# Compact head operands, padded on chip: the operand staging of an attention and MLP training kernel

## The chip, the cores and the metric

The kernel runs on one core of one Trainium2 chip. The metric is the device time of one execution in microseconds (us). A run is an execution of its own, and a kernel's time is the median of its runs.

Engines are named as the profile names them: PE is the matrix engine (PEld its weight loads), DVE the vector engine, ACT the scalar engine, POOL is GpSimd, SP is the engine that only issues DMAs. The recorded texts also say VectorE for DVE, ScalarE for ACT, GpSimd for POOL and SyncE for SP. ACTq and SPq are the instructions by which ACT and SP issue DMAs. PSUM is where this kernel's matmuls put their results, and an *eviction* is the copy of such a result by DVE or ACT to a tile that other operations or DMAs read. The *granted clock* of PE is the share of its full clock that the profile shows as let through.

## The reference, cut to what matters

The reference computes the output and all gradients of one block that multiplies attention by a gate from an MLP:

```python
x  = A_x                                  # [1, 2048, 512] bf16
xn = layernorm(x)
q, k, v = split(xn @ wqkv)                # 32 heads of 16 columns
s  = softmax(q k^T / 4) v @ wo            # attention
g  = silu(gelu(layernorm(xn) @ w1 + b1) @ w2 + b2)   # MLP, 1792 wide
out = x + s * g
# returned: out and the gradients of x, wqkv, wo, w1, b1, w2, b2 for a given grad_out
```

## The kernel before

The kernel has three parts. The *preparation* normalizes x, computes K and V, then Q, then the MLP with its gate, and projects the gradient of the attention output through `wo` (`do_proj`). The *attention* works on 16 pairs of heads, in 4 blocks of queries with 16 steps each, 1024 steps in all. The *gradient part* does the rest.

The attention wants, for each pair, K with V, Q, and the projected gradient (call it DO) with columns on partitions. The kernel before gets these by DMA transposes that read a scratch in DRAM. In that scratch each pair has 128 columns per tile of 128 rows: two heads of 64, each holding `1 or -norm | 16 columns | 16 columns | 31 zeros`. So the preparation fills two staging tiles `KP` with zeros once, writes the live columns into them, and stores them whole, zeros too, 1 MB for two tiles of rows.

```python
# K/V stage (two KP tiles, used in turn)
KP = [stg.tile([128, NPAIR, 2, 128], bf16, name=f"KP{i}") for i in range(2)]
for i in range(2):
    nc.gpsimd.memset(KP[i][:], 0.0)
    ...
for t in range(NT):                       # 16 tiles of 128 rows
    ...                                   # 8 matmuls: pk, pv
    nc.vector.tensor_copy(out=kpv[:, :, :, 1:17], in_=pk...)
    nc.scalar.copy(out=kpv[:, :, :, 17:33], in_=pv...)
    if t % 2 == 1:
        (nc.sync if (t // 2) % 2 == 0 else nc.scalar).dma_start(out=k.KVsrc[...], in_=kp[:])
    nc.vector.tensor_tensor(out=sq..., in0=kk, in1=kk, op=ALU.mult)     # squares of K
    nc.vector.reduce_sum(out=kn2[:], in_=sq[:], axis=AX.X)
    nc.vector.tensor_tensor(out=kmaxrun[:], in0=kmaxrun[:], in1=kn2[:], op=ALU.max)
nc.gpsimd.partition_all_reduce(kmax2[:], kmaxrun[:], channels=128, reduce_op=bass_isa.ReduceOp.max)

# Q stage: the same two tiles
QP = KP
for i in range(2):
    nc.gpsimd.memset(QPv[:, :, :, :, 17:33], 0.0)
for t in range(NT):
    ...                                   # 4 matmuls: pq; cast into QP; copy to NQ; squares, sum, norm
    if t % 2 == 1:
        (nc.sync if (t // 2) % 2 == 0 else nc.scalar).dma_start(out=k.QTsrc[...], in_=qp[:])

# MLP stage, once per tile t of 128 rows (ps_m: 14 matmuls)
nc.vector.tensor_tensor(out=m_bf[:], in0=pm[:], in1=b2bc[:], op=ALU.add)
nc.scalar.activation(out=sg[:], in_=m_bf[:], func=ACT.Sigmoid)
nc.vector.tensor_tensor(out=gB[:, 0, :], in0=m_bf[:], in1=sg[:], op=ALU.mult)
nc.scalar.dma_start(out=dot[:], in_=go2[t * 128:(t + 1) * 128, :])
nc.vector.tensor_tensor(out=dso[:], in0=dot[:], in1=gB[:, 0, :], op=ALU.mult)
...                                       # dso to DRAM; transposed by PE, copied to dsoT by ACT
nc.gpsimd.tensor_scalar(out=q[:], in0=sg[:], ...)      # three POOL operations
nc.gpsimd.tensor_tensor(out=q[:], in0=q[:], in1=gB[:, 0, :], op=ALU.mult)
nc.gpsimd.tensor_tensor(out=q[:], in0=q[:], in1=sg[:], op=ALU.add)
nc.vector.tensor_tensor(out=gB[:, 1, :], in0=q[:], in1=dot[:], op=ALU.mult)
nc.scalar.dma_start(out=k.GB_s[t * 128:(t + 1) * 128, :, :], in_=gB[:])
if t >= 1:
    do_proj(t - 1)

def do_proj(t):
    ...                                   # 4 matmuls: pd
    nc.vector.tensor_copy(out=dpv[:, :, :, 17:33], in_=pd...)
    nc.scalar.copy(out=nd[:, :, t % 4, :]..., in_=pd...)
    if t % 4 == 3:
        nc.scalar.dma_start(out=k.NATQd_s[...], in_=nd[:])
    if t % 2 == 1:
        (nc.sync if (t // 2) % 2 == 0 else nc.scalar).dma_start(out=k.DOTsrc[...], in_=dp[:])

# attention, operands of one pair (all issued by SP)
eng.dma_start_transpose(out=t["KVT"]..., in_=KVT_s[p]...)   # from KVsrc in DRAM
eng.dma_start_transpose(out=t["QT"]...,  in_=QT_s[p]...)
eng.dma_start_transpose(out=t["DOT"]..., in_=DOT_s[p]...)
...                                       # three plain loads
```

The program text is not the order of execution on an engine. A scheduler in the build puts the instructions of each engine into one fixed sequence, and the engine then runs that sequence in order.

## Time and profile before

The time before was 3028.48 us, the median of four runs (3026.97 to 3030.4). The profiled execution took 3025.2 us.

The table of windows of the kernel before gives one row per stage, cut at events read from the timeline: first K/V eviction, last K tile, last Q tile, first matmul of the MLP's second layer (`ps_m`), last eviction of `pd`, first `gts` (the first full attention step), last `acc` (end of attention). Evictions are those by DVE. The columns are start and end of the window, its length, busy time and number of instructions of PE, PEld, DVE, ACT and POOL, the granted PE clock as a share of full speed, the busy share of the DMA engines, and GB/s.

```profile
67.00:104.10 37.10, 30.44 (x126) 13.10 (x129) 31.51 (x67) 9.27 (x17) 8.60 (x5) 0.88 0.78 214
104.10:155.80 51.70, 26.27 (x88) 9.85 (x90) 39.01 (x89) 19.83 (x40) 1.43 (x2) 0.79 0.71 187
155.80:176.50 20.70, 17.54 (x76) 7.66 (x75) 14.71 (x23) 14.95 (x24) 6.96 (x2) 0.86 0.68 216
176.50:305.20 128.70, 101.67 (x455) 44.08 (x463) 70.83 (x110) 49.77 (x80) 50.76 (x50) 0.91 0.54 163
305.20:323.60 18.40, 2.50 (x12) 0.82 (x14) 0.02 (x1) 3.91 (x4) 0.34 (x2) 0.50 1.09 270
323.60:2421.60 2098.00, 1894.21 (x16637) 562.20 (x16634) 1545.61 (x1664) 1936.39 (x2046) 195.06 (x574) 1.00 0.82 148
2421.60:3025.20 603.60, 412.83 (x2370) 212.25 (x2410) 299.69 (x419) 163.72 (x259) 259.23 (x224) 0.87 0.39 119
```

Attention is 69% of the span, and ACT is busy 92% of it (1936 of 2098 us). The change acts before attention, in some 320 us. There no engine is busy all through a row; DVE comes nearest in the first (31.51 of 37.10 us), and PE in the third (17.54 of 20.70). The fifth row, the start of attention, is 18.4 us in which nearly nothing computes.

The list of waits of the kernel before, for 60 to 156 us, shows what the K/V and Q stages wait for. Columns: engine, what it was about to write and on which line, what released it; total us, number of waits, longest.

```profile
POOL KP L156 <- DMA KVsrc<-KP: 28.1, 1, 28.1
ACT NQ L167 <- DVE KP L164: 21.6, 9, 5.1
PE pq L160 <- DVE KP L164: 19.4, 6, 9.2
...
DVE KP L164 <- DMA QTsrc<-KP: 10.4, 4, 4.0
...
POOL kmax L151 <- DVE sqq L171: 6.1, 1, 6.1
```

POOL's zero fill of the tiles for Q waits for the last K/V writes (the 28.1 us are POOL's idle time, mostly free). PE waits 19.4 us for DVE to evict Q, and DVE waits 10.4 us for the 1 MB writes that still read the two staging tiles.

### The profile page before, as it was taken

The numbers are of one execution on the slowest core, as the hardware profiler recorded it, in microseconds if no ns is written. First come the engines' busy times: TensorE is split into PE (matmuls) and PEld (weight loads), VectorE is DVE, ScalarE is ACT, GpSimd is POOL, SyncE is SP. The second block draws the span as 40 slices with busy tenths as digits, with TensorE's granted clock in tenths as the row PEclk, the third lists the DMA queues.
The fourth block names the chain that finished last, engine by engine and source line by source line (L and its number), as shares of the span: only waits on it lengthen the run. The fifth ranks groups of instructions, "written<-read, shape, count | busy, mean of one in ns | idle before, by whom it ended". The sixth has DMA issues, their size and how long they took to land. (4 is left out here: it accounts for less than half of the span.)

```text
span 3025.2 us, 50085 instructions
## 1 busy us (share of the span) xinstructions
PE 2506.4 (83%) x19909; PEld 864.8 (29%) x19968; DVE 2035.1 (67%) x2470; ACT 2217.1 (73%) x2503; POOL 523.5 (17%) x867
## 2 busy tenths in 40 slices
PE   3678698998998998998998999899899865665967
PEld 2233222222222222222222222222222233332443
DVE  5855577777777777777777777777777637882034
ACT  2344699999999999999999999999999924441020
POOL 1043001001001001001001001001000126881024
PEclk8889899999999999999999999999999988887989
DMA  5855978878887887878788798878867663325431
GB/s 168 218 178 171 186 139 155 149 146 163 130 166 146 148 151 143 166 134 161 147 147 159 135 167 142 152 147 147 163 131 136 105 220 105 102 81 149 129 124 42
DMA packets 1365582, 442.27 MB, mean 146 GB/s; under 512 B 1247714, under 2 KB 1349475, under 8 KB 1365347
## 3 DMA queue, kind: packets, MB, share of 16 engines
q1 hardware_dynamic: 1267186, 374.04, 63.7%
q10 hardware_dynamic: 98160, 65.02, 7.2%
q8 instruction: 156, 2.56, 0.4%
q14 instruction: 80, 0.65, 0.1%
HBM read 69.34 MB, written 76.03 MB: 48 GB/s over the span
## 5 line engine op out<-in xcount | busy, mean ns | idle before, releaser
L698 DVE TENSOR_TENSOR gts<-d,et 128x1024 bf16<-128x1024 f32 x1024 | 1251.9, 1223 | 547.7 <-ACT et L687 524.2
L687 ACT ACTIVATE et<-s 128x1024 bf16<-128x1024 f32 x1024 | 1050.2, 1026 | 163.4 <-PE s L644 128.4
L724 ACT ACTIVATE e<-t 128x1024 bf16<-128x1024 f32 x1024 | 1049.7, 1026 | 6.3 <-PE t L656 5.1
L656 PE MATMUL t<-KVT,QT 64*128 64x512 bf16 x2048 | 400.8, 379 | 127.0 <-ACT e L724 122.6
L820 PE MATMUL Z<-e,W 128*32 128x512 bf16 x2048 | 396.2, 381 | 45.9 <-POOL W L787 45.9
L667 PE MATMUL d<-DOT,KVT 64*128 64x512 bf16 x2048 | 401.1, 380 | 18.0 <-DVE gts L698 9.3
L644 PE MATMUL s<-QT,KVT 64*128 64x512 bf16 x2048 | 401.3, 388 | 13.8 <-DMA QT<-QTsrc 12.4
L739 PE MATMUL X<-et,Lc 128*32 128x512 bf16 x2048 | 403.3, 389 | 2.4 <-DVE xt L772 0.4
L824 PE MATMUL Z<-gk,W 128*32 128x512 bf16 x2048 | 400.5, 379 | 0.0
L755 PE MATMUL X<-gts,NAT 128*17 128x512 bf16 x2048 | 395.6, 381 | 0.0
L742 PE MATMUL X<-et,NAT 128*32 128x512 bf16 x2048 | 395.2, 391 | 0.0
L781 POOL TENSOR_TENSOR W<-NATQ,rL 128x128 bf16<-128x128 bf16 x64 | 25.7, 402 | 1892.2 <-DVE rL L780 1892.2
L656 PEld LDWEIGHTS <-QT 64*128 64x128 bf16 x2048 | 179.1, 94 | 374.2 <-issue 373.9
L667 PEld LDWEIGHTS <-KVT 64*128 64x128 bf16 x2048 | 180.8, 93 | 265.1 <-issue 249.1
L644 PEld LDWEIGHTS <-KVT 64*128 64x128 bf16 x2048 | 100.9, 93 | 441.8 <-issue 440.3
L739 PEld LDWEIGHTS <-Lc 128*32 128x32 bf16 x2048 | 100.5, 93 | 243.9 <-issue 235.5
L820 PEld LDWEIGHTS <-W 128*32 128x32 bf16 x2048 | 118.9, 96 | 107.0 <-POOL W L787 64.4
L832 DVE TENSOR_TENSOR acc<-Z,acc 64x512 f32<-64x512 f32 x192 | 129.2, 673 | 8.7 <-PE Z L824 8.7
L824 PEld LDWEIGHTS <-W 128*32 128x32 bf16 x2048 | 105.6, 96 | 76.6 <-issue 3.3
L755 PEld LDWEIGHTS <-NAT 128*17 128x17 bf16 x2048 | 94.6, 88 | 11.5 <-issue 4.9
L742 PEld LDWEIGHTS <-NAT 128*32 128x32 bf16 x2048 | 95.0, 94 | 1.1 <-issue 1.1
L437 PE MATMUL dh_tp<-ident_bf,dh 128*128 128x128 bf16 x224 | 29.2, 263 | 77.1 <-DVE dh L434 74.7
(198 smaller groups left out, 2548.2 us busy)
## 6 DMA issues: line engine op xcount, KB each, us to landing
NAT<-KVsrc SPq DMA_DIRECT2D x16, 512.0 KB, 4.5
gk<-gts SPq DMA_TRANSPOSE x512, 4.3
HG_s<-hg SPq DMA_DIRECT2D x16, 448.0 KB, 2.8
DH_s<-dh ACTq DMA_DIRECT2D x16, 448.0 KB, 2.5
KVsrc<-KP SPq DMA_DIRECT2D x4, 1024.0 KB, 5.7
KVsrc<-KP ACTq DMA_DIRECT2D x4, 1024.0 KB, 5.7
QTsrc<-KP SPq DMA_DIRECT2D x4, 1024.0 KB, 5.2
QTsrc<-KP ACTq DMA_DIRECT2D x4, 1024.0 KB, 8.0
```

What stands on the lines that cost most here:

```text
L644: nc.tensor.matmul(s[:, hj, :], lhsT=op["KVT"][r0:r0 + 64, kb * 128:(kb + 1) * 128], rhs=op["QT"][r0:r0 + 64, qc * 512:(qc + 1) * 512], st ...
L656: nc.tensor.matmul(t[:, hj, :], lhsT=op["QT"][r0:r0 + 64, q0:q0 + 128], rhs=op["KVT"][r0:r0 + 64, kc * 512:(kc + 1) * 512], start=True, st ...
L667: nc.tensor.matmul(d[:, hj, :], lhsT=op["KVT"][r0:r0 + 64, kb * 128:(kb + 1) * 128], rhs=op["DOT"][r0:r0 + 64, qc * 512:(qc + 1) * 512], s ...
L687: nc.scalar.activation(out=et, in_=st_s.pop(g)[:], func=ACT.Exp)
L698: nc.vector.tensor_tensor(out=gts[:, kb % 2], in0=st_d.pop(g)[:], in1=st_et[g], op=ALU.mult)
L724: nc.scalar.activation(out=e[:], in_=st_t.pop(g)[:], func=ACT.Exp)
L739: nc.tensor.matmul(X[64 + 32 * hj:64 + 32 * hj + 32, :], lhsT=Lc[:, :], rhs=et[:, hj, :], start=(kb == 0), stop=False, skip_group_check=Tr ...
L742: nc.tensor.matmul(X[32 * hj:32 * hj + 32, :], lhsT=NATt[:, kb, 64 * hj + 1:64 * hj + 33], rhs=et[:, hj, :], start=(kb == 0), stop=(kb == ...
L755: nc.tensor.matmul(X[64 + 32 * hj:64 + 32 * hj + 17, :], lhsT=NATt[:, kb, 64 * hj:64 * hj + 17], rhs=gts[:, kb % 2, hj, :], start=False, s ...
L820: nc.tensor.matmul(Z[32 * hj:32 * hj + 32, :], lhsT=W1[:, qb, hj, :], rhs=erhs, start=(qb == 0), stop=False, tile_position=(0, 32 * hj))
L824: nc.tensor.matmul(Z[32 * hj:32 * hj + 32, :], lhsT=W2[:, qb, hj, :], rhs=grhs, start=False, stop=(qb == 3), tile_position=(0, 32 * hj))
L832: nc.vector.tensor_tensor(out=av, in0=Z[0:64, :], in1=av, op=ALU.add)
```

## The change

The intent is to keep the zeros out of DRAM. K/V, Q and DO go to DRAM compact; the attention loads them compact, copies them into padded tiles on chip, and transposes from there.

1. K/V: two staging tiles of four row tiles, 33 columns per head instead of 64. A write is 1.08 MB for four row tiles instead of 2 MB, in runs of 528 bytes. K is evicted by ACT, V by DVE, and the squares move from DVE to ACT. The big zero fill is gone. The pool of the small work tiles gets a third buffer (`p15_wk`).
2. Q: four staging tiles instead of the two shared ones, 17 columns per head, runs of 272 bytes; no second, padded copy; evicted by ACT.
3. `do_proj`: the padded eviction and the 1 MB `DOTsrc` writes are dropped. DVE makes the compact copy that ACT made.
4. Attention: three padded tiles, filled by POOL copies, and transposes from them; a third `NAT` buffer (K with V, rows on partitions); the PSUM pools of X and Z are put ahead of that of d.

The diff, cut to its core:

```diff
-            wk = c0.enter_context(tc.tile_pool(name="p15_wk", bufs=2))
+            wk = c0.enter_context(tc.tile_pool(name="p15_wk", bufs=3))
-            KP = [stg.tile([128, NPAIR, 2, 128], bf16, name=f"KP{i}") for i in range(2)]
+            NS = [stg.tile([128, NPAIR, 4, 2, NATW], bf16, name=f"NS{i}") for i in range(2)]
             for i in range(2):
-                nc.gpsimd.memset(KP[i][:], 0.0)
 ...
-            NQ = [stg.tile([128, NPAIR, 4, 32], bf16, name=f"NQ{i}") for i in range(2)]
+            NQ = [stg.tile([128, NPAIR, 4, 2, 17], bf16, name=f"NQ{i}") for i in range(4)]
 ...
-                nc.vector.tensor_copy(out=kpv[:, :, :, 1:17], in_=pk...)
-                nc.scalar.copy(out=kpv[:, :, :, 17:33], in_=pv...)
-                if t % 2 == 1:
-                    (nc.sync if ... else nc.scalar).dma_start(out=k.KVsrc[...], in_=kp[:])
+                nc.scalar.copy(out=kpv[:, :, :, 1:17], in_=pk...)
+                nc.vector.tensor_copy(out=kpv[:, :, :, 17:33], in_=pv...)
+                if t % 4 == 3:
+                    (nc.sync if ... else nc.scalar).dma_start(out=k.NAT_s[...], in_=ns...)
-                nc.vector.tensor_tensor(out=sq..., in0=kk, in1=kk, op=ALU.mult)
+                nc.scalar.activation(out=sq..., in_=kk, func=ACT.Square)
 ...
-            QP = KP
-            for i in range(2):
-                nc.gpsimd.memset(QPv[:, :, :, :, 17:33], 0.0)
 ...
-                nc.vector.tensor_copy(out=qpv[:, :, :, 1:17], in_=pq...)
+                nq = NQ[t // 4]
+                nc.scalar.copy(out=qpv[:, :, :, 1:17], in_=pq...)
-                nc.scalar.copy(out=nq[:, :, t % 4, :]..., in_=qq)
 ...                                     (do_proj)
-                nc.vector.tensor_copy(out=dpv[:, :, :, 17:33], in_=pd...)
-                nc.scalar.copy(out=nd[:, :, t % 4, :]..., in_=pd...)
+                nc.vector.tensor_copy(out=nd[:, :, t % 4, :]..., in_=pd...)
-                if t % 2 == 1:
-                    (nc.sync if ... else nc.scalar).dma_start(out=k.DOTsrc[...], in_=dp[:])
 ...                                     (attention)
+    KPad = opnd.tile([128, 16, 2, 64], bf16, name="KPad")     (QPad, DPad alike)
+    nc.gpsimd.memset(KPad[:], 0.0)                            (QPad, DPad alike)
-        ops.append(lambda: eng.dma_start_transpose(out=t["KVT"]..., in_=KVT_s[p]...))
+        def tk():
+            nc.gpsimd.tensor_copy(out=KPad[:, :, :, 0:NATW], in_=t["NAT"][:])
+            eng.dma_start_transpose(out=t["KVT"]..., in_=KPad...)
 ...                                     (tq and td alike, after the plain loads)
```

## The prediction

> **What bounds the kernel now.** The table of windows splits the 3025 us into preparation (to 304 us), start of attention (to 323.6), attention (to 2430) and gradient phase. In attention ACT is busy 92%, PE 90%, DVE 74%, DMA 82%. A step takes 2.03 us (two exponentials of 1.026 us), and the list of waits shows no wait of PE, ACT or DVE for a DMA there. The instruction order on PE, ACT and DVE is the same in both kernels from the second block of attention on, so I expect that unchanged; the change acts in the first 324 us.
>
> **What it removes and moves.**
> 1. K/V stage (67 to 103.3). In the timeline the first eviction waits for a 3.5 us POOL memset of KP; the new one covers 128 columns. Per tile DVE does cast, square, reduce (0.69 + 0.69 + 0.68 us); square moves to ACT, leaving DVE about 1.3 and ACT 1.2. PE needs 8 matmuls of 0.215 and is nearly the limit already. About 7 us off, 3.5 of it the memset.
> 2. Q stage (103.3 to 156). DVE waits 10.4 us for QTsrc writes to leave KP; their 1 MB holds the pace to two tiles per 8 to 11 us. The new stage has a buffer for every four tiles, so no eviction waits for a DMA. DVE then does about 1.5 us a tile, 24 us, once the partition maximum is there (about 103.5). End near 131, with 3 fewer h1 tiles done (2.6 us to pay back). With the stalls at 156 to 164 the first MLP matmul (176.5 now) comes 25 to 28 us earlier, item 1 included.
> 3. MLP stage (176.5 to 304). Its 5.5 us period runs through ACT sg, three POOL ops (0.85 + 1.2 + 1.15), DVE gB and the GB_s issue on ACT's queue. The removed work lies beside it: 0 to 4 us.
> 4. Start of attention. QT lands 12.3 us after 304.1 and DOT 18.7, held up by DOTsrc writes (DMA share 1.02). After: three pad memsets (1.75 us each, half of the 3.5 for 128x4096) and a 128x1056 copy (estimate 1.5) precede the K transpose; NATQd must be written, loaded, copied, transposed (4.3). s at 12 to 13 us as now, d at 13.5: 5 us less.
> 5. In attention POOL gets three copies per pair (about 3 us of 131; it is 9% busy), clear of the finalization in the order. SyncE has some 15% to spare. No effect.
>
> The Trainium skill (DMA: Bandwidth & Descriptors, Specifications) gives 512 B as the smallest transfer at line rate; the new Q runs are 272 B, but nothing waits for them.
>
> **Sum.** 27 + 2 + 5 = 34 us: 2994 us, 8 in 10 between 2976 and 3012. Faster by over 2%: 0.07; within 2%: 0.91; slower: 0.02.
>
> **What will show it.** First K/V eviction at about 67.2 us; no wait for a DMA of the Q staging tiles; first MLP matmul near 150; gts starting about 14 us later; 2106 us from there to the end of attention, within 5.
>
> **What would make it wrong.** Attention moving: PSUM places of X, Z and d are exchanged, and 1% of a step is 21 us. SyncE stalling on pad copies so that gk transposes come late. A low granted PE clock in the Q stage (0.67 to 0.83 there now). Transposes from on-chip memory being dearer than from DRAM.

## The result, and the profile after

The changed kernel takes 2978.39 us, the median of 8 runs (2974.91 to 2980.89), against 3028.83 us for the kernel before in the same rounds (13 runs, 3026.97 to 3030.98). The ratio is 0.9832, with a 95% interval from 0.9823 to 0.9842. A ratio is the mean time of one kernel's fast runs over that of the other's of the same rounds, so it is not quite the ratio of the medians quoted beside it. The gain of 50.4 us is 1.7%, within the 2% line. Both kernels give correct results.

The table of windows of the changed kernel, cut at the same events, with the same columns:

```profile
67.20:94.60 27.40, 26.51 (x114) 11.74 (x117) 22.59 (x49) 19.26 (x33) 1.18 (x2) 0.92 0.43 119
94.60:122.50 27.90, 20.02 (x85) 8.72 (x85) 25.92 (x71) 15.44 (x36) 0.46 (x1) 0.88 0.44 109
122.50:142.20 19.70, 18.61 (x91) 8.54 (x91) 16.39 (x26) 15.95 (x26) 0.35 (x2) 1.00 0.56 175
142.20:256.90 114.70, 93.26 (x455) 41.49 (x463) 65.66 (x110) 41.90 (x65) 51.82 (x49) 0.98 0.37 120
256.90:273.20 16.30, 1.37 (x6) 0.49 (x7) 0.04 (x1) 2.31 (x2) 8.89 (x10) 0.50 0.99 228
273.20:2370.20 2097.00, 1893.72 (x16642) 560.09 (x16640) 1545.21 (x1664) 1938.14 (x2047) 228.52 (x617) 1.00 0.83 146
2370.20:2973.10 602.90, 413.05 (x2370) 211.43 (x2410) 299.61 (x419) 164.00 (x259) 259.43 (x224) 0.86 0.39 119
```

The stages set side by side, in us, with what the prediction gave for each:

| stage | before | changed | difference | predicted |
|---|---|---|---|---|
| start to first K/V eviction | 70.58 | 67.17 | -3.4 | -3.5 |
| first K/V eviction to last K tile | 33.54 | 27.40 | -6.1 | -3.5 |
| last K tile to partition maximum ready | 7.12 | 0.81 | -6.3 | none |
| to the last Q tile | 44.54 | 27.11 | -17.4 | (see below) |
| to the first `ps_m` matmul | 20.72 | 19.72 | -1.0 | |
| *sum, to the first `ps_m` matmul* | *176.50* | *142.21* | *-34.3* | *-25 to -28* |
| MLP stage, to the last `pd` eviction | 128.70 | 114.73 | -14.0 | 0 to -4 |
| start of attention, to the first `gts` | 18.38 | 16.29 | -2.1 | -5 |
| attention | 2098.0 | 2097.0 | -1.0 | 0 |
| gradient part | 603.6 | 602.9 | -0.7 | 0 |
| profiled execution | 3025.2 | 2973.1 | -52.1 | -34 |

In the first row of the table of windows PE is now busy 26.51 of 27.40 us: the K/V stage is PE-bound. In the second DVE is busy 25.92 of 27.90 us: the Q stage is DVE-bound. And the biggest surprise is the fourth row. PE does the same 455 instructions in the MLP stage, at 0.98 of full clock instead of 0.91, in 14 us less, although the change hardly touches that stage's chain of work.

The list of waits of the changed kernel, 60 to 142 us, to be held against the one above:

```profile
POOL kmax L150 <- DVE kmaxrun L148: 26.3, 1, 26.3
...
ACT NQ L159 <- PE pq L155: 2.9, 9, 0.7
```

No wait names a DMA of the Q staging tiles any more, and PE's 19.4 us wait for the eviction of Q is gone.

### The profile page after: what moved, and what is told of

It is laid out like the page before. It is cut to its first block, busy times and chain, and to the rows that moved or that the text cites. A ratio compares the mean times of both kernels' runs of the same rounds, so it can differ in the third digit from the quotient of the medians.

```text
span 2973.1 us, 50093 instructions
## 1 busy us (share of the span) xinstructions
PE 2486.9 (84%) x19909; PEld 856.9 (29%) x19968; DVE 2009.2 (68%) x2438; ACT 2216.2 (75%) x2501; POOL 551.8 (19%) x912
## 3 DMA queue, kind: packets, MB, share of 16 engines
HBM read 65.41 MB, written 55.32 MB: 41 GB/s over the span
## 5 line engine op out<-in xcount | busy, mean ns | idle before, releaser
L786 POOL TENSOR_TENSOR W<-NATQd,rL 128x128 bf16<-128x128 bf16 x64 | 25.7, 402 | 1517.5 <-DVE rL L785 1517.5
```

## The experiments

Twelve kernels were run, in three batches of four; all gave correct results. A batch shares its runs of the kernel before: their median was 3029.48 us in the first (7 runs), 3027.38 in the second (7) and 3029.97 in the third (9). "Against before" below is the difference of medians within a batch. Every kernel was timed in 4 or 5 runs, and one profile of each gave the stages. Two profiles of kernels with the same instruction order in the MLP stage differed there by up to 3 us, so smaller differences of one stage between single profiles carry no argument unless other runs repeat them.

### The MLP stage: traffic, work, or order?

The table of windows says only that the stage is 14 us shorter. The change removes three things from it: an eviction per tile, 8.4 MB of `DOTsrc` writes, and the issues of those writes on the queues of SP and ACT.

The timeline shows where the time sat. Normally a tile's `m_bf` is followed on DVE by the same tile's `gB`, and tiles follow each other every 5.5 us. In the kernel before, DVE's instruction order has three places where two `m_bf` stand before the first one's `gB`. Written as a sequence, `m` for `m_bf` and `g` for the product `gB<-m_bf,sg`, over the 16 tiles:

```
before:          mgmgmgmgmgmmggmgmgmmggmgmgmmggmg
changed kernel:  mgmgmgmgmgmgmgmgmgmgmgmgmgmgmgmg
```

This is the instruction order of the built programs, not a measurement. What a doubled place costs is seen in the timeline of the kernel before (start, length, engine, line, operation; in brackets the idle time before it, and what ended it):

```profile
208.08 0.69 DVE L242 TENSOR_TENSOR m_bf<-ps_m,b2bc 128x512 bf16<-128x512 f32 x1
209.14 0.63 ACT L244 ACTIVATE sg<-m_bf 128x512 bf16<-128x512 bf16 x1 [2.60 <-DVE m_bf L242]
...
211.14 0.69 DVE L242 TENSOR_TENSOR m_bf<-ps_m,b2bc 128x512 bf16<-128x512 f32 x1 [1.77 <-PE ps_m L239]
211.74 0.41 DVE L246 TENSOR_TENSOR gB<-m_bf,sg 128x512 bf16<-128x512 bf16 x1
...
217.76 0.58 ACT L56 COPY dsoT<-tp_ps 128x512 bf16<-128x512 bf16 x1 [4.07 <-DMA GB_s<-gB]
...
218.37 4.05 PE L239 MATMUL ps_m<-w_sb,hgT 128*128 128x512 bf16 x9
...
223.90 0.69 DVE L242 TENSOR_TENSOR m_bf<-ps_m,b2bc 128x512 bf16<-128x512 f32 x1 [4.58 <-PE ps_m L239]
```

The first tile's `sg` is ready at 209.77, but DVE must first do the second `m_bf`, which waits 1.77 us for PE; the first `gB` starts at 211.74. Everything behind it is late: the POOL operations of both tiles run back to back, and the second tile's `gB` and `dso` take DVE 1.32 and 1.37 us (much the same at all three places), where most take 0.4 to 0.7. ACT is idle 4.07 us before its second `dsoT` copy. The bracket names a `GB_s` write, but the copy starts when PE has made what it copies: the second `dso` ends at 217.07, PE's transposes of it at 217.73, the copy starts at 217.76. PE has little to do from 212 to 218 us (busy 1.88 of 6.00), and its next 9 matmuls take 4.05 us, 0.43 us apart, where 14 of them took 3.19 us at 207.91. The Trainium skill ("TensorE: Matmul & The Clock Gate", "What's actually happening") says that the PE clock falls to half after an idle window of about 3.4 us. The trace agrees on the half rate: the granted clock is 0.50 for 6.8 us after each doubled place, here from 216.19 to 223.01. It does not show that much idle time before it: in the 3.41 us before the drop PE was busy 0.90 us.

The order of PE and ACT changes at these places too, not only DVE's. In the plain order a tile's 14 `ps_m` matmuls stand 8 before and 6 behind the transposes of the tile before, so that PE has work while it waits for ACT and DVE. At a doubled place all 14 stand ahead, then the transposes of both tiles, each with half of one projection behind it and no `ps_m` matmul between; ACT has both `sg` before the first tile's `dsoT`. "Doubled" below means this whole order.

The changed kernel at a place that answers to it has the plain order. From its timeline:

```profile
161.36 0.68 DVE L226 TENSOR_TENSOR m_bf<-ps_m,b2bc 128x512 bf16<-128x512 f32 x1
162.41 0.63 ACT L228 ACTIVATE sg<-m_bf 128x512 bf16<-128x512 bf16 x1 [2.59 <-DVE m_bf L226]
163.07 0.42 DVE L230 TENSOR_TENSOR gB<-m_bf,sg 128x512 bf16<-128x512 bf16 x1 [0.43 <-ACT sg L228]
...
166.87 0.68 DVE L226 TENSOR_TENSOR m_bf<-ps_m,b2bc 128x512 bf16<-128x512 f32 x1
```

Here `gB` starts 0.66 us after the start of `sg`, and the next `m_bf` is 5.51 us after the last.

The theory was that the instruction order costs the time, and that the order comes from the `DOTsrc` writes issued on ACT's queue. The rivals were that the traffic of the writes costs it, or the extra eviction. Four kernels built from the changed one get the old `do_proj` back, in whole or in part; its `DOTsrc` is then written but never read, so the result stays right.

**m_full.** The changed kernel with all of the old `do_proj`.

```diff
+            DP = [dstg.tile([128, NPAIR, 2, 128], bf16, name=f"DP{i}") for i in range(2)]   # zero-filled
+                nc.vector.tensor_copy(out=dpv[:, :, :, 17:33], in_=pd...)
-                nc.vector.tensor_copy(out=nd[:, :, t % 4, :]..., in_=pd...)
+                nc.scalar.copy(out=nd[:, :, t % 4, :]..., in_=pd...)
+                if t % 2 == 1:
+                    (nc.sync if (t // 2) % 2 == 0 else nc.scalar).dma_start(out=k.DOTsrc[:, :, t - 1:t + 1, :]..., in_=dp[:])
```

> The changed kernel with the old projection step put back: DP evicted by VectorE, ND by ScalarE, DOTsrc written from both queues, but read by nobody. The MLP stage (first ps_m matmul to last eviction of pd) took 128.0 us before and 114.0 after. The instruction order of this kernel has three places where two m_bf stand before the gB of the first, as before had and after has not. Theory 'order': three such places at about 4.8 us each: stage 127 to 129 us, total 13 to 16 us over the changed kernel (about 2992). Theory 'state' (the stage got faster because the stages ahead of it leave fewer DMAs behind): stage stays near 114, total near 2979.

Measured: 2995.02 us (2992.81 to 2996.12), ratio 0.9888 [0.9874, 0.9903]. The built order has the three doubled places again, exactly as before, and the MLP stage takes 125.4 us (a little under the 127 to 129 expected), the start of attention 22.3; the total is 34.5 us against before. So most of the surprise comes with `do_proj`, whatever else has changed earlier.

**m_sync.** As m_full, but all `DOTsrc` writes are issued by SP.

```diff
-                    (nc.sync if (t // 2) % 2 == 0 else nc.scalar).dma_start(out=k.DOTsrc[...], in_=dp[:])
+                    nc.sync.dma_start(out=k.DOTsrc[...], in_=dp[:])
```

> As the one with the old projection step, but all DOTsrc writes are issued by SyncE. Same bytes, same evictions; the instruction order has none of the three doubled places. Theory 'order': stage 114 to 117 us, total 2979 to 2985. Theory 'traffic' (8 MB of extra writes contend with the loads and writes of the stage): stage near 128, total near 2992.

Measured: 2983.55 us (2981.02 to 2984.3), ratio 0.985 [0.9835, 0.9865], 11.5 us less than m_full with the same work and the same bytes. No doubled place is left in the order; the MLP stage takes 120.3 us, above the 114 to 117 of theory 'order', so the order is not all of it.

**m_half.** As m_full, with both queues, but only pairs 0 to 7 are written.

```diff
-                    (nc.sync if ...).dma_start(out=k.DOTsrc[:, :, t - 1:t + 1, :]..., in_=dp[:])
+                    (nc.sync if ...).dma_start(out=k.DOTsrc[0:8, :, t - 1:t + 1, :]..., in_=dp[:, 0:8])
```

> As the one with the old projection step, but only 8 of the 16 pairs are written, so half the bytes; writes on both queues; the three doubled places are in the order. Theory 'order': stage 127 to 129 us, as with all bytes; total 2990 to 2994. Theory 'traffic': about half of the 14 us, stage near 121, total near 2985.

Measured: 2993.61 us (2991.44 to 2996.6), ratio 0.9885 [0.9871, 0.99]: the same as m_full within the intervals. The order has the three doubled places, and the stage takes 128.2 us. Half of the traffic gives nothing; moving all of it to the other queue gives 11.5 us.

**m_nowrite.** As m_full without any `DOTsrc` write; both evictions stay.

```diff
-                if t % 2 == 1:
-                    (nc.sync if ...).dma_start(out=k.DOTsrc[...], in_=dp[:])
```

> The changed kernel with both evictions of pd put back (DP by VectorE, ND by ScalarE) but DP never written. No doubled place in the order. The MLP stage took 114.7 us in the changed kernel and 120.3 with evictions and all writes from SyncE. Theory 'evictions' (ND on ScalarE waits for DP and stands ahead of the next sg): stage 119 to 121, total 2982 to 2985. Theory 'traffic': the 5.6 us were the writes; stage 114 to 116, total 2978 to 2981.

Measured: 2980.87 us (2978.05 to 2982.48), ratio 0.9845 [0.9831, 0.986]. The plain order, and a stage of 114.1 us, like the changed kernel's 114.7. The extra eviction costs nothing that shows in this stage. The writes do, in the stage: 120.3 us with them (m_sync) and 114.1 without. One place shows how. In the timelines of m_sync and then of m_nowrite, at the same tile:

```profile
173.90 1.85 ACTq L250 DMA_DIRECT2D GB_s<-gB  x1
175.85 0.63 ACT L236 ACTIVATE sg<-m_bf 128x512 bf16<-128x512 bf16 x1 [3.61 <-DVE DP L197]
```

```profile
173.02 0.33 ACTq L248 DMA_DIRECT2D GB_s<-gB  x1
173.69 0.63 ACT L234 ACTIVATE sg<-m_bf 128x512 bf16<-128x512 bf16 x1 [2.32 <-DVE m_bf L232]
```

While the DMA engines are full (busy share 0.99 from 170 to 176 us, against 0.68 in m_nowrite), the issue of one write stays on ACT's queue 1.85 us instead of 0.33, and `sg` starts 1.39 us after the end of its `m_bf` (at 174.46) instead of 0.10. Over the stage the 40 issues on ACT's queue take 18.9 us in m_sync and 14.6 in m_nowrite. The releaser named in the bracket of m_sync, a DVE eviction, is not what `sg` needs; it is only the event that came last. In total time the two kernels, of different batches, are not told apart: 0.985 and 0.9845. m_nowrite gains some 4 us less than the changed kernel (46.5 against 50.4, with intervals that overlap); its start of attention took 19.9 us.

**b_sync.** The test in the other direction: the kernel before with one word changed.

```diff
-                    (nc.sync if (t // 2) % 2 == 0 else nc.scalar).dma_start(out=k.DOTsrc[...], in_=dp[:])
+                    nc.sync.dma_start(out=k.DOTsrc[...], in_=dp[:])
```

> The kernel before with one word changed: all DOTsrc writes are issued by SyncE. No byte and no operation less; the three doubled places vanish from the order. Theory 'order': MLP stage 114 to 117 us instead of 128, total 3013 to 3017 (before 3028.5). Theory 'traffic' or 'evictions': no change, 3026 to 3031.

Measured: 3018.25 us (3017.81 to 3021.93), ratio 0.997 [0.9953, 0.9986], 11.2 us against before. All bytes, all work and the padded layout are still there. The doubled places are gone from the order; the MLP stage takes 119.7 us and the start of attention 15.1. Theory 'order' had said 114 to 117 us and 3013 to 3017 in all; it missed them by 3 and 1 us, having counted nothing for the writes.

How the parts add up is best seen at the three doubled places alone. The next table sums, from the timelines, the six intervals between starts of `m_bf` that they cover (tiles 6 to 8, 10 to 12 and 14 to 16), in us:

| kernel | order | `DOTsrc` written | sum of the six intervals | MLP stage |
|---|---|---|---|---|
| before | doubled | all, both queues | 47.4 | 128.7 |
| m_full | doubled | all, both queues | 45.5 | 125.4 |
| m_half | doubled | half, both queues | 47.1 | 128.2 |
| b_sync | plain | all, SP only | 37.8 | 119.7 |
| m_sync | plain | all, SP only | 37.6 | 120.3 |
| m_nowrite | plain | none | 33.8 | 114.1 |
| changed kernel | plain | none | 33.7 | 114.7 |

The order is worth 47.4 - 37.8 = 9.6 us and the writes another 37.8 - 33.7 = 4.1 us: together 13.7 of the stage's 14.0. Each is one profile against one; with the three kernels of the next sections that keep the old writes (b_zero 45.7 and b_q4 46.4, doubled; b_q4_sync 37.2, plain), the order is worth 8 to 10 us. The bytes do not grade the doubled rows at all. Nor is it the time of the four issues themselves: each takes 0.4 us on ACT's queue. The runs do not separate the parts of the new order (DVE's, ACT's, PE's, and the half PE clock that comes with it). Why the scheduler doubles at those places was not looked into. What is shown is that it does so when the `DOTsrc` issues stand on ACT's queue, and not when they stand on SP's.

### The partition maximum

The Q norms need the maximum of K's norms over all partitions, made by one POOL instruction. In the kernel before it was ready (and scaled by DVE) 7.12 us after the last K tile, in the changed one 0.81 us. From the timeline of the kernel before:

```profile
102.69 1.02 POOL L156 MEMSET KP<- 128x1024 bf16 x1 [28.08 <-DMA KVsrc<-KP]
103.93 0.19 DVE L149 TENSOR_TENSOR kmaxrun<-kmaxrun,kn 128x32 f32<-128x32 f32 x1
109.78 0.45 POOL L151 PARTITION_ALL_REDUCE kmax<-kmaxrun  x1 [6.06 <-DVE sqq L171]
```

and of the changed kernel:

```profile
94.38 0.19 DVE L148 TENSOR_TENSOR kmaxrun<-kmaxrun,kn 128x32 f32<-128x32 f32 x1
94.71 0.46 POOL L150 PARTITION_ALL_REDUCE kmax<-kmaxrun  x1 [26.33 <-DVE kmaxrun L148]
```

In the kernel before its input is complete at 104.12, and POOL is free at 103.71, yet the reduction starts at 109.78. The Trainium skill ("GPSIMD Engine Reference", "Instruction dispatch") says that the first call of a freshly loaded POOL kernel pays a load of about 6 us that shows as no instruction. The 6.06 us here agree. The traces also hold two records named MODIFY_POOL_CONFIG at the reduction's line, which the timeline view leaves out: in the kernel before they end at 103.71, in the changed kernel at 68.04. The changed kernel fits: there POOL has nothing else in its queue, reaches the reduction early, and the load hides in the 26 us wait for K. The releaser in the first bracket, a DVE square of Q, is wrong. Two kernels test this, and what it is worth.

**a_pool.** The changed kernel, with a tiny POOL copy that has to wait for the last K tile put in front of the reduction.

```diff
+            kmaxc = big.tile([128, H], f32, name="kmaxc")
+            nc.gpsimd.tensor_copy(out=kmaxc[:], in_=kmaxrun[:])
-            nc.gpsimd.partition_all_reduce(kmax2[:], kmaxrun[:], ...)
+            nc.gpsimd.partition_all_reduce(kmax2[:], kmaxc[:], ...)
```

> The changed kernel with one small GpSimd copy of kmaxrun (128x32) ahead of the reduction, so that the set-up instruction of the reduction stands behind it in GpSimd's queue instead of waiting there early. In the changed kernel the reduction ended 0.8 us after the last K tile, before the change 7.1 us after. Theory 'set-up': the maximum comes 6.5 to 7.5 us after the last K tile. The order lets VectorE do about 4.3 us of Q squares meanwhile, so the total rises by 1 to 4 us only (2980 to 2983). Rival (the 6 us were a wait for VectorE): at most 1.5 us.

```profile
95.02 0.21 POOL L151 COPY kmaxc<-kmaxrun 128x32 f32<-128x32 f32 x1 [26.57 <-DVE kmaxrun L148]
102.23 0.45 POOL L152 PARTITION_ALL_REDUCE kmax<-kmaxc  x1 [7.00 <-issue]
```

Measured: 2978.18 us (2975.11 to 2981.35), ratio 0.9837 [0.9823, 0.9852]. The gap is back, 7.00 us in the timeline above, behind the MODIFY_POOL_CONFIG records at 95.2, and this time the profile finds no releaser for it. But the time is the changed kernel's, under the 2980 to 2983 expected. From the last K tile to the last Q tile it took 29.2 us instead of 27.9, for DVE did the squares and sums of Q meanwhile, which need no maximum.

**b_zero.** The kernel before, with the fill of the Q tiles on DVE, so that POOL's queue is free.

```diff
-                nc.gpsimd.memset(QPv[:, :, :, :, 17:33], 0.0)
+                nc.vector.memset(QPv[:, :, :, :, 17:33], 0.0)
```

> The kernel before, with the two fills of KP between the K/V and the Q loop done by VectorE instead of GpSimd. Theory 'queue' (the reduction over partitions waits on GpSimd behind a fill that waits for the KVsrc writes, and for 6 us of set-up that then comes after it): the maximum is there within 1 us of the last K tile plus a fill or two, near 106 instead of 111.2. If the Q stage hangs on the maximum, its end comes 4 to 6 us earlier and the total is 3023 to 3025; if the Q stage hangs on its QTsrc writes, its end stays near 155.8 and the total at 3026 to 3031. I expect the second.

Measured: 3026.61 us (3025.64 to 3027.47), ratio 0.9997 [0.998, 1.0013]. The maximum was ready 0.81 us after the last K tile, 6 us earlier, and the last Q tile came 1.1 us earlier, at 154.6 us. The wait was real, it was found and removed, and it was worth nothing clear of the noise, as expected: the Q stage before was held by something else.

### The Q stage: bytes or buffers?

**b_q4.** The kernel before with four Q staging tiles instead of two, and all bytes as they were.

```diff
+            QX = [stg.tile([128, NPAIR, 2, 128], bf16, name=f"QX{i}") for i in range(2)]   # zero-filled
-            QP = KP
+            QP = KP + QX
-                qp = QP[(t // 2) % 2]
+                qp = QP[(t // 2) % 4]
```

> The kernel before with four Q staging tiles in turn instead of two; the same bytes are written. Q stage 44.5 us from the maximum to the last tile (27.1 in the changed kernel). Theory 'buffers' (an eviction waits until its tile has been written): 8 to 14 us shorter, total 3014 to 3021. Theory 'bytes' (10 MB of Q writes at some 200 GB/s bind the stage): less than 4 us, total 3024 to 3030.

Measured: 3018.56 us (3016.19 to 3020.83), ratio 0.9971 [0.9956, 0.9985], 8.8 us against before. From the maximum to the last Q tile it took 32.9 us instead of 44.5. DVE's wait for `QTsrc` writes fell from 10.4 to 1.9 us. So it was the two tiles that held the stage at 44.5 us, and not the bytes as such. What holds it at 32.9 is not tested: DVE is busy 28.97 us of it, and the busy share of the DMA engines is 0.96. The changed kernel's stage is 27.1 us, with a DVE cast less per tile; there DVE is busy 25.71 us, and the DMA share is 0.43.

### Both placements in the kernel before

**b_q4_sync.** The kernel before with the edits of b_q4 and b_sync.

```diff
+            QX = ...                             # as in b_q4
-            QP = KP
+            QP = KP + QX
-                qp = QP[(t // 2) % 2]
+                qp = QP[(t // 2) % 4]
-                    (nc.sync if (t // 2) % 2 == 0 else nc.scalar).dma_start(out=k.DOTsrc[...], in_=dp[:])
+                    nc.sync.dma_start(out=k.DOTsrc[...], in_=dp[:])
```

> The kernel before with both placement edits: four Q staging tiles, and DOTsrc writes from SyncE alone. It moves every byte that before moves. Alone they gave 8.8 and 11.2 us; if they are independent, 3006 to 3010. What is then left to the changed kernel, some 30 us, is work and bytes that it removed.

Measured: 3008.09 us (3006.38 to 3010.76), ratio 0.9929 [0.9915, 0.9942], 21.9 us against before; the two alone gave 8.8 + 11.2 = 20.0. So about 40% of the changed kernel's 50.4 us is to be had with every padded byte still written, by one more pair of buffers and one word.

### The start of attention

Here the change gained 2.1 us where 5 were predicted. From the timeline of the kernel before:

```profile
316.45 0.61 PE L644 MATMUL s<-QT,KVT 64*128 64x512 bf16 x2 [12.39 <-DMA QT<-QTsrc]
322.87 1.03 PE L667 MATMUL d<-DOT,KVT 64*128 64x512 bf16 x4 [3.54 <-DMA DOT<-DOTsrc]
```

and of the changed kernel:

```profile
256.33 1.80 POOL L580 MEMSET KPad<- 128x2048 bf16 x1 [1.12 <-PE pd L190]
...
261.63 1.09 POOL L602 COPY KPad<-NAT 128x1056 bf16<-128x1056 bf16 x1
262.58 0.32 SPq L598 DMA_DIRECT2D NATQd<-NATQd_s  x1
263.00 1.95 SPq L603 DMA_TRANSPOSE KVT<-KPad  x1
265.04 2.21 SPq L608 DMA_TRANSPOSE QT<-QPad  x1
267.30 2.88 SPq L613 DMA_TRANSPOSE DOT<-DPad  x1
...
272.44 1.03 PE L670 MATMUL d<-DOT,KVT 64*128 64x512 bf16 x4 [1.65 <-DMA DOT<-DPad]
```

Three pad fills of 1.80 us and the pad copies stand one behind the other on POOL, and on SP the load of the last gradient columns stands ahead of the three transposes. The first matmul with DO still starts 15.5 us after the last `pd` eviction (256.94 to 272.44). The prediction had the pieces but summed them to 13.5 us. b_sync and b_q4_sync, which still transpose from DRAM, need only 15.1 and 15.2 us for this stage; the changed kernel, a_pool and p_psum 16.3, 16.0 and 16.2. So the on-chip route was not the faster one here. Why the stage became shorter at all in the changed kernel no run isolates: m_nowrite, also without `DOTsrc`, took 19.9 us for it.

**s_early.** The changed kernel with the first pair's operand tiles and the pads put at memory that is free already in the MLP stage, so that their fills, K and Q can be done there.

```diff
+    padp = ctx.enter_context(tc.tile_pool(name="padp", bufs=1))
+    padp.tile([128, 3840], bf16, name="hole")
+    opn0 = ctx.enter_context(tc.tile_pool(name="opn0", bufs=1))
 ...
+        pl = opn0 if i == 0 else opnd            # KVT, QT, DOT, NATQq, NATQd of pair 0; NAT0; the pads
```

> The changed kernel with the first pair's operand tiles and the three pads placed where memory is free during the MLP stage, so that pads, loads and the K and Q transposes of pair 0 are done there. From the last eviction of pd to the first gts took 16.3 us. Theory 'chain' (the DOT chain write, load, copy, transpose is what lasts): s runs early, d and gts at 11 to 13 us; total 2973 to 2976. Theory 'queue' (the prefetch transposes of pair 1, which stand ahead of NATQd and DOT in SyncE's queue, set the time): gts at 15 to 18 us, total 2977 to 2981.

Measured: 2982.59 us (2980.75 to 2983.1), ratio 0.9842 [0.9828, 0.9855]. That is theory 'queue', though the total was a little above its range. The first `s` can start early, but `gts` still came 16.5 us after the last `pd` eviction: the transposes for the *second* pair were now ahead of the first pair's DO in SP's queue.

**s_fence.** As s_early, with three one-column copies that make the second pair's loads wait for the first `gts`.

```diff
+        if g == 0:
+            for tl in (NAT3[1]..., OP[1]["NATQq"]..., OP[1]["NATQd"]...):     # one column each
+                nc.vector.tensor_copy(out=tl, in_=st_gt[0][:, 0, 0, 0:1])
```

> As the one with early operands, and the loads of pair 1 are made to depend on the first gts by three one-column copies, so that nothing stands ahead of NATQd and DOT of pair 0. Both theories: gts 10 to 12 us after the last eviction of pd; total 2971 to 2975. If gts stays at 15 us or more, the write and load of NATQd themselves are the chain and were taken too short.

Measured: 2980.58 us (2977.64 to 2980.78), ratio 0.9835 [0.9821, 0.9848]. The start of attention fell from 16.5 us in s_early to 12.4, so the queue was the reason there. But the total, expected at 2971 to 2975, is the changed kernel's, for the stretch from the last Q tile to the first `ps_m` matmul grew from 19.7 to 23.3 us (23.1 in s_early). The early loads and transposes share SP's queue with the writes of the MLP's first layer (`H1T_s`), and the waits of DVE for these writes in that stretch grew from 2.2 us to 7.8 in s_early and 8.2 in s_fence. No kernel of the twelve beat the changed one clear of the noise.

### The PSUM pools

**p_psum.** The changed kernel with the PSUM pools in their old order. The prediction had named this exchange as the main danger.

```diff
+    ps_d = ctx.enter_context(tc.tile_pool(name="ps_dt", bufs=2, space=PSUM))
+    ps_t = ps_d
     ps_x = ...
     ps_z = ...
-    ps_d = ctx.enter_context(tc.tile_pool(name="ps_dt", bufs=2, space=PSUM))
-    ps_t = ps_d
```

> The changed kernel with the PSUM pools in the old order. The attention stage took 2098.0 us before and 2097.0 after; I expect 2096 to 2099 and the total within 2 us of the changed kernel; if the places of X, Z and d matter, the step changes and 1% would be 21 us.

Measured: 2978.91 us (2977.64 to 2980.01), ratio 0.9831 [0.9818, 0.9845]; attention took 2097.7 us. The places make no difference.

## Why the prediction was right or wrong

The class was right (within 2%), and the time of 2978.39 us lies in the range of 2976 to 3012, near its lower end. The gain was 50.4 us where 34 were forecast. Of the profile's 52.1 us, the prediction's sum lacked 7 us before the MLP and 12 us in it, and had 3 us too many at the start of attention. The two larger misses point the same way; that the time still fell inside is owed to the width of the range, not to the sum.

- **Step 1, K/V stage, "about 7 us off, 3.5 of it the memset": right in mechanism, a little small.** The first eviction came at 67.17 us (67.2 predicted), and the stage gave 9.5 us in all. PE is busy 26.51 of 27.40 us there, so it is at the limit that the step named.
- **Step 2, Q stage: the mechanism was right, and shown by b_q4; the size was short.** "No eviction waits for a DMA" held. "End near 131" was 8.5 us late. The step let DVE's 24 us begin "once the partition maximum is there (about 103.5)". The maximum was ready at 95.4, because a free POOL queue hides the load in front of the reduction, which the prediction had not looked up. But a_pool shows that a late maximum alone (102.9) costs only 1.3 us: DVE goes on with squares and sums. To let all of DVE's work begin after the maximum was the error.
- **Step 3, MLP stage, "the removed work lies beside it: 0 to 4 us": this is the step that failed.** It measured 14.0 us. That the eviction lies beside the chain was right (m_nowrite: 114.1 us with it, 114.7 without). The step failed because it took the 5.5 us period as what sets the stage's time. Three places of the kernel before ran at an average of 7.9 us a tile (47.4 over six), because the built order had two `m_bf` ahead of a `gB`; m_sync, m_half and b_sync tie that to the queue that issued `DOTsrc`, worth 8 to 10 us at these places. The traffic of `DOTsrc`, which the step had not counted in this stage, was worth another 4.1 us there by the profiles. The prediction compared the built order of the two kernels for attention and found it unchanged; it says nothing of the order in this stage, where the sequence of `m_bf` and `gB` would have shown it before any run.
- **Step 4, start of attention, "5 us less": wrong in size.** It measured 2.1 us. DO's first matmul came 15.5 us after the last `pd` eviction instead of 13.5; the sum left out a wait of 2.1 us: DO's copy ended at 265.19, and its transpose was issued at 267.30, behind those of K and Q on SP. With the fills and K and Q done early and SP's queue cleared (s_fence), 3.9 us of the stage go (16.3 to 12.4); the early fills alone gave nothing (s_early, 16.5).
- **Step 5, attention, "no effect": right.** It took 2098.0 us before and 2097.0 after (the prediction's 2106 us runs to a later mark than the last `acc`); in the twelve experiments 2096.7 to 2100.4. The feared exchange of PSUM places did nothing (p_psum).
- **The 272-byte runs.** The prediction cited the Trainium skill ("DMA: Bandwidth & Descriptors", "Specifications") for 512 bytes as the smallest transfer at line rate, and said that nothing would wait for the shorter runs. Nothing did: no wait in the Q stage names their DMA. No run here shows what the shorter runs themselves cost, nor the 512 bytes.

What stays open: why the scheduler doubles; how the 6 us that m_sync's stage loses against m_nowrite's divide between slow issues and PE clock; and how the remaining 28.5 us of gain (50.4 - 21.9) divide in total time between bytes and removed work. By stages, the profile puts it into the K/V stage, the last part of the Q stage and the MLP's writes. No run isolates the 9.5 us of the K/V stage. From the other side, m_full loses 15.9 us of the gain (50.4 - 34.5) by the old `do_proj` alone.

## What to carry to other kernels

When a change moves or removes DMAs, compare the built instruction order of the stages around them, not only of the longest stage: a DMA issue is an instruction on an in-order engine, and here one word that chose its engine, and the order that the scheduler then built, was worth 11.2 us with every byte kept. Count a removed wait as gain only after asking what the waiting engine would do next: the maximum that came 6 us earlier gained nothing, since two staging tiles held the stage. And before crediting a new layout with a gain, give the old one the buffers and queues of the new: here that alone gave some 40%.

## What the Trainium skill lacked or had wrong

- "Trainium Kernel Development and Optimization", "Key Constraints", says that issuing DMAs from several engines only saves the sequencer's issue time. Here the choice of engine for four writes moved the total from 3029.48 to 3018.25 us, with the built order of DVE, ACT and PE changed by it, while the four issues themselves take 0.4 us each. The page does not mention that side.
- "Perfetto Trace Analysis", "DMA Instruction — HWDGE (DVE, Sync)", explains that the record of a DMA issue covers the wait for the descriptor generator, but gives no durations. The same issue on ACT's queue took 0.33 us in one run and 1.85 us where the DMA engines were 0.99 busy, and ACT's next operation came 1.3 us later.
- "GPSIMD Engine Reference", "Instruction dispatch", gives about 6 us for the first call of a freshly loaded kernel; the runs agree at 6.06 us and show 7.00 once. It does not say that the load hides where POOL reaches the instruction before its operands are ready: 0.81 us from the last K tile to the maximum, against 7.12. Nor does it say that a profile may name a false releaser for this gap, as it did here (a DVE square that the reduction does not read).
- "TensorE: Matmul & The Clock Gate", "HAM oscillation — how this bites in real kernels", gives the rule of no PE gaps over about 3.4 us. Here PE dropped to half rate (9 matmuls, 0.43 us apart) though it had been busy 0.90 us of the 3.41 us before the drop, and no single gap in the profile was over 2.77 us. The rule did not suffice. The page's next section does tell of a kernel whose frequent short pauses had this effect, but it gives no length for them.
